# Hash attention and a gated feed-forward block: turning the first pair's second half of queries behind the first scores

## The chip, the cores and the metric

The kernel runs on one core of one Trainium2 chip. The metric is the device time of one execution in microseconds (us). The profile is of one execution; its times run from the first instruction of the span. TensorE is PE in the profile (its weight loads PEld), VectorE is DVE, ScalarE is ACT, GpSimd is POOL, SyncE, which issues most of the DMAs, is SP.

## The reference

Attention in which a query sees only the keys of its own hash bucket, and a feed-forward block behind it, all in 32-bit floats:

```python
q, k, v: (4, 8, 768, 64); proj: (64, 6); w_in: (512, 2048); w_out: (2048, 512)
q_bits = (einsum('bhsd,dk->bhsk', q, proj) > 0)      # six signs for a query, and k_bits for a key
mask = q_bucket[:, :, :, None] == k_bucket[:, :, None, :]
scores = where(mask, 1/sqrt(64) * q @ k.T, -1e9)
attn = softmax(scores)                               # with 1e-9 added to the sum
x = (attn @ v) as (3072, 512)
h = x @ w_in
out = (h / (1 + exp(-1.702 * h))) @ w_out            # (3072, 512)
```

## The kernel before, in words

Attention runs first, over 16 pairs of heads: a pair holds two heads of 64 rows each, so together they fill the 128 partitions. The sequence of 768 is cut into two halves `c` of 384 queries (`HS`) and six tiles `kt` of 128 keys; `GT` is 3, and `low` and `high` are key tiles 0 to 2 and 3 to 5. The feed-forward block behind it forms its matrix products from seven products of quarters with sums around them (L712 and L824 are its matmuls). A second, general version of the attention stands under a condition at the end and isn't taken here.

The order of the instructions on TensorE, VectorE, ScalarE and GpSimd is the order in which the code issues them (`manual_schedule`); the framework adds the waits. SP's DMA queue has its own order, which is the same in both kernels.

What the change touches is the start. `first_pair` handles pair 0, whose data are laid out in another way than the later pairs':

- It loads `k`, `proj` and `q` on the queues of SP and ScalarE, and lets TensorE run four `warm` matmuls (L359) meanwhile. `hash_weights` (L130, L133) makes the hash weights `pf_k` and `pf_q` from `proj` on VectorE.
- `turned(name, c, move)` turns a half of the keys or queries with matmuls against the identity (`tp`, L366: six matmuls, which the profile shows as 12 records), and the function `move` copies the result into `kT` or `qT` (L368). For `k` that is VectorE, for `q` ScalarE.
- `bits(name, c)` multiplies a half with the hash weights (`hash`, L373), and VectorE turns the signs into the features `kf` or `qf` (L374).
- `measure` (L398) sums the squares of a raw tile on ScalarE; a guard uses them at the end.

Then `scores(n, c, kts)` makes a score tile `ps` for each key tile (L432): two bf16 matmuls with the features, which add a large number where a bit agrees, and two 32-bit ones with `qT` and `kT`, one for each head. ScalarE takes the exponential into `e` (L433). `add_low` (L440, L441, POOL) and `add_high` (L446, L448, VectorE) sum the exponentials in `acc`, `values` multiplies them with `v` (`av`, L458), and `unload` (L469, L470) copies the result. From pair 1 on, `fetch` (L328) loads keys and queries, `turn` (L391) transposes them on VectorE, and `hashed` (L408) and `featured` (L413, with DMAs at L420 that bring the features into place) do the hashing.

Two sets of buffers tie these steps together. The pool `sps` has three score buffers in PSUM, used in turn by every `tp` of pair 0, every `hash` of pair 0 and every `ps`: a new one has to wait until the engine that reads the one three before it is done. And the raw queries of a pair have one buffer (pool `ld`, one buffer for each name), so `fetch(1, "q")` can't start before the last reader of pair 0's raw queries.

The main sequence, before:

```python
rest = first_pair()
fetch_v(0)
for x in "kq":
    fetch(1, x)
scores(0, 0, low)
rest()
```

Of the kernel before, what the change touches and what calls it, by code (L numbers as in the profile page):

```python
# [38 lines left out]
def kernel(  # L39
# [17 lines left out]
    nc = tc.nc  # L57
# [65 lines left out]
    def hash_weights():  # L123
        for x in "kq":
            for j in range(2):
                rows = slice(D * j, D * (j + 1))
                for h, sign in enumerate(SIGNS[x]):
                    c0 = NB * (2 * j + h)

                    nc.vector.scalar_tensor_tensor(pf[x][rows, c0 : c0 + NB], pj[rows], sign, ones[rows, 0:NB],  # L130
                                                   op0=Alu.mult, op1=Alu.mult)
            w, one = (y[:, 0 : 4 * NB].rearrange("p (j n) -> p j n", j=2) for y in (pf[x], ones))
            nc.vector.tensor_tensor(pf0[x][:, :, 0 : 2 * NB], w, one, op=Alu.mult)  # L133
# [149 lines left out]
    def attention(ff):  # L283
# [4 lines left out]
        with actx:  # L288
# [41 lines left out]
            def fetch_v(n):  # L330
                b, hp = pairs[n]
                x = ld.tile([P, T, 2, D], F32, tag="v", name="v", bufs=2)
                if n == 0:
                    x = x.rearrange("p t j d -> p (t j d)").rearrange("p (j t d) -> p t j d", j=2, d=D)
                vts[n] = x
                if n == 1:
                    behind(x[:, 0, :, 0])
                for j in range(2):
                    order = "(t p) d -> p t d" if n else "(p t) d -> p t d"
                    loader[0].dma_start(out=x[:, :, j, :], in_=v[b, 2 * hp + j].rearrange(order, p=P))  # L340

            def first_pair():


                b, hp = pairs[0]
                x = {}
                for i, (name, src) in enumerate((("k", k), ("q", q))):
                    raw = raws[0, name] = ld.tile([P, S // 32, 32], F32, tag=name, name=name)
                    x[name] = raw.rearrange("p s i -> p (s i)").rearrange("p (j t d) -> p j t d", j=2, d=D)
                    for j, queue in enumerate((nc.sync, nc.scalar)):  # L350
                        queue.dma_start(out=x[name][:, j], in_=src[b, 2 * hp + j].rearrange("(p t) d -> p t d", p=P))
                    if i == 0:
                        for j, queue in enumerate((nc.sync, nc.scalar)):
                            queue.dma_start(out=pj[D * j : D * (j + 1)], in_=proj)
                    xts[0, name] = wk.tile([P, S], F32, tag=f"{name}T", name=f"{name}T")

                nc.scalar.activation(const.tile([1, 1], F32, name="first"), ones[0:1, 0:1], Act.Exp)
                for _ in range(4):
                    nc.tensor.matmul(aps.tile([P, 512], F32, tag="av", name="warm"), idle[:, 0:P], idle, start=True, stop=True)  # L359
                hash_weights()  # L360

                def turned(name, c, move):
                    tp = sps.tile([P, 2, 512], F32, tag="s", name="tp")[:, 0, 0:HS]
                    for i in range(GT):
                        for j in range(2):
                            nc.tensor.matmul(tp[D * j : D * (j + 1), i * P : (i + 1) * P], x[name][:, j, c * GT + i, :], ident,  # L366
                                             start=True, stop=True)
                    move(xts[0, name][:, c * HS : (c + 1) * HS], tp)  # L368

                def bits(name, c):  # L370
                    cols = slice(c * HS, (c + 1) * HS)
                    h = sps.tile([P, 2, 512], F32, tag="s", name="hash0")[:, 0, 0:HS]
                    nc.tensor.matmul(h, pf0[name].rearrange("p j d -> p (j d)"), xts[0, name][:, cols], start=True, stop=True)  # L373
                    nc.vector.tensor_scalar(feats[0][name][:, cols], h, above0[name][:, 0:1], FEAT[name],  # L374
                                            op0=Alu.is_gt, op1=Alu.mult)

                measure(0, "k")
                turned("k", 0, nc.vector.tensor_copy)
                turned("k", 1, nc.vector.tensor_copy)
                turned("q", 0, nc.scalar.copy)  # L380
                turned("q", 1, nc.scalar.copy)
                measure(0, "q")
                bits("k", 0)
                bits("q", 0)
                bits("k", 1)
                return lambda: bits("q", 1)

            def turn(n, name):
                x = raws[n, name]
                xt = xts[n, name] = wk.tile([P, S], F32, tag=f"{name}T", name=f"{name}T")  # L390
                nc.vector.transpose(xt, x.rearrange("p s i -> p (s i)"))  # L391

            def measure(n, name):

                x = raws.pop((n, name))
                i = 2 * n + "kq".index(name)
                junk = st.tile([P, S], BF16, tag="junk", name="junk", bufs=1)
                nc.scalar.activation(junk, x.rearrange("p s i -> p (s i)"), Act.Square, accum_out=sizes[:, i : i + 1])  # L398
# [24 lines left out]
            def scores(n, c, kts):  # L423
                qT, kT, qf, kf = xts[n, "q"], xts[n, "k"], feats[n % 2]["q"], feats[n % 2]["k"]
                cols = slice(c * HS, (c + 1) * HS)
                for kt in kts:
                    ps = sps.tile([P, 2, 512], F32, tag="s", name="ps")
                    keys = slice(kt * P, (kt + 1) * P)
                    for a, m, last in ((kf, qf, False), (kT, qT, True)):
                        for j in range(2):  # L430
                            hs = slice(D * j, D * (j + 1))
                            nc.tensor.matmul(ps[:, j, 0:HS], a[hs, keys], m[hs, cols], start=not last, stop=last)  # L432
                    nc.scalar.activation(es[c][:, kt, :, 0:HS], ps[:, :, 0:HS], Act.Exp, scale=1.0 / D**0.5)  # L433
# [3 lines left out]
            def add_low(n, c):  # L437

                acc = accs[n, c, 0] = st.tile([P, 2, HS], F32, tag="acc0", name="acc0", bufs=1)
                nc.gpsimd.tensor_tensor(acc, es[c][:, 0, :, 0:HS], es[c][:, 1, :, 0:HS], op=Alu.add)  # L440
                nc.gpsimd.tensor_tensor(acc, acc, es[c][:, 2, :, 0:HS], op=Alu.add)  # L441
# [81 lines left out]


            low, high, every = range(GT), range(GT, T), range(T)
            rest = first_pair()
            fetch_v(0)
            for x in "kq":
                fetch(1, x)
            scores(0, 0, low)  # L530
            rest()
            add_low(0, 0)
            scores(0, 0, high)
            turn(1, "k")
            measure(1, "k")
            values(0, 0, low)
# [442 lines left out]

    ff = feed_forward("", in_chunks[len(in_chunks) - LATE :])  # L980
    attention(ff)
    whole(ff)
    fixed.close()
# [41 lines left out]
```

## Time and profile before

| what | value |
|---|---|
| time, median of 4 runs | 875.17 us (874.86 to 875.98) |
| the profiled execution | 875.0 us; its span 873.2 us |
| granted TensorE clock | 0.996 |
| TensorE matmuls | 861.7 us busy, 99% of the span |
| VectorE, ScalarE, GpSimd | 82%, 36%, 37% of the span |
| first score matmul (L432) | starts at 10.47 us |
| first values matmul (L458) | starts at 16.38 us |

The times of a timeline row are its start and its length; a row can merge several instructions (x12 means twelve). In square brackets stands how long the engine had been idle before, and who released it. The ends of matmuls are modelled, so rows of TensorE that follow each other overlap a little. The chain of waits is the chain of work that ended last, followed back from the end of the program; its pieces don't overlap, and "issue" in it is time in which an engine waited for nothing that the profile shows.

### The profile page before, as it was taken

The page shows a single profiled execution, that of the slowest core. Times are in us where ns is not written, and L with a number is a line of the kernel's source. Part 1 is how long each engine was busy: PE and PEld are TensorE (multiplying, and loading weights), DVE is VectorE, ACT ScalarE, POOL GpSimd, SP SyncE. Part 2 cuts the span into 40 slices and gives each one's busy share as a digit, 9 for nine tenths or more (in the row PEclk, how much of TensorE's full clock was granted, in tenths as well). Part 3 has the DMA queues.
Part 4 walks back from the last instruction along what each step waited for, and adds up shares of the span by engine and source line. Part 5 has one row for each costly group of instructions (what it writes and reads, how often), then busy time and mean ns, then how long its engine had stood idle before and what let it go on. Part 6 is the DMA issues. An engine that isn't in the chain of part 4 may idle for free.

```text
span 873.2 us, 11818 instructions
## 1 busy us (share of the span) xinstructions
PE 861.7 (99%) x4077; PEld 500.7 (57%) x4077; DVE 718.7 (82%) x1020; ACT 311.6 (36%) x519; POOL 321.2 (37%) x275
## 2 busy tenths in 40 slices
PE   9999999999999999999999999999999999999995
PEld 4444444444444444444444444444888888888884
DVE  4579999988999988778777778888888977897785
ACT  5756567777666653222233222332000000000000
POOL 4243334334433375665543344659903100000000
PEclk9999999999999999999999999999999999999998
DMA  5334456554445304565455545575844685467524
GB/s 133 59 59 84 84 104 101 116 88 83 84 84 91 75 25 158 192 217 193 175 193 186 205 180 196 190 251 179 299 168 156 199 247 197 166 200 241 193 97 99
DMA packets 169155, 131.99 MB, mean 151 GB/s; under 512 B 123616, under 2 KB 138112, under 8 KB 163712
## 3 DMA queue, kind: packets, MB, share of 16 engines
q1 hardware_dynamic: 166528, 129.70, 51.2%
q10 hardware_dynamic: 2560, 1.46, 0.7%
q8 instruction: 34, 0.56, 0.3%
q14 instruction: 33, 0.27, 0.1%
HBM read 79.69 MB, written 50.33 MB: 149 GB/s over the span
## 4 chain that ended last, share of the span: by engine, by line
PE 95%; DVE 3%; DMA 0%; issue 0%; ACT 0%; ACTq 0%; SPq 0%; DVEq 0%
PE product L712 33%; PE product L824 27%; PE ps L432 18%; PE av L458 14%; PE dn L479 1%; PE hash L408 1%; DVE xT L828 1%; DVE y L804 1%; DMA pj<-in_proj_dram 0%; DVE acc L448 0%; DVE xT L499 0%; PE hash L373 0%; DVE acc L446 0%; ACT e L433 0%; DVE v L828 0%
## 5 line engine op out<-in xcount | busy, mean ns | idle before, releaser
L433 ACT ACTIVATE e<-ps 128x768 f32<-128x768 f32 x192 | 150.2, 812 | 17.0 <-PE ps L432 14.9
L432 PE MATMUL ps<-qT,kT 64*128 64x384 f32 x768 | 155.1, 482 | 0.0
L712 PE MATMUL product<-xT,w_in_sb 128*128 128x512 f32 x288 | 135.4, 592 | 0.0
L458 PE MATMUL av<-e,v 128*64 128x385 f32 x768 | 128.2, 488 | 0.0
L440 POOL TENSOR_TENSOR acc<-e 128x768 f32<-128x768 f32 x32 | 51.2, 1599 | 192.2 <-ACT e L433 122.6
L720 ACT ACTIVATE c<-c 128x512 f32<-128x512 f32 x72 | 45.3, 630 | 185.0 <-issue 78.6
L458 PEld LDWEIGHTS av<-e,v 128*64 128x64 f32 x768 | 53.8, 136 | 72.9 <-issue 72.0
L712 PEld LDWEIGHTS product<-xT,w_in_sb 128*128 128x128 f32 x288 | 54.6, 190 | 69.0 <-issue 64.0
L712 PE MATMUL product<-t_x,s_in 128*128 128x512 f32 x192 | 90.2, 592 | 0.0
L432 PEld LDWEIGHTS ps<-qT,kT 64*128 64x128 f32 x768 | 68.0, 187 | 38.0 <-issue 37.5
L219 POOL TENSOR_TENSOR v<-c,u 128x512 f32<-128x512 f32 x24 | 34.1, 1422 | 121.2 <-ACT c L720 121.2
L837 ACT COPY u<-product 128x256 f32<-128x256 f32 x21 | 7.8, 372 | 172.1 <-PE product L824 138.9
L441 POOL TENSOR_TENSOR acc<-acc,e 128x768 f32<-128x768 f32 x32 | 64.0, 2001 | 2.5
L432 PE MATMUL ps<-qf,kf 64*128 64x384 bf16 x384 | 62.8, 324 | 0.1
L712 PEld LDWEIGHTS product<-t_x,s_in 128*128 128x128 f32 x192 | 36.5, 190 | 45.9 <-issue 43.8
L446 DVE SCALAR_TENSOR_TENSOR acc<-e 128x768 f32<-128x768 f32 x32 | 50.6, 1582 | 5.1 <-ACT e L433 5.1
L712 PE MATMUL product<-t_x,w_in_sb 128*128 128x512 f32 x96 | 45.1, 592 | 0.0
L712 PE MATMUL product<-xT,s_in 128*128 128x512 f32 x96 | 45.1, 592 | 0.0
L432 PEld LDWEIGHTS <-kf 64*128 64x128 bf16 x384 | 19.3, 94 | 35.2 <-issue 11.7
L448 DVE TENSOR_TENSOR acc<-acc,acc 128x768 f32<-128x768 f32 x32 | 31.2, 974 | 4.8 <-POOL acc L441 1.6
L824 PE MATMUL product<-raw_g,xT 128*128 128x256 f32 x152 | 35.1, 379 | 0.0
L448 DVE TENSOR_TENSOR acc<-acc,e 128x768 f32<-128x768 f32 x32 | 31.8, 995 | 3.8 <-ACT e L433 0.5
(207 smaller groups left out, 1494.0 us busy)
## 6 DMA issues: line engine op xcount, KB each, us to landing
raw_g<-g_dram SPq DMA_DIRECT2D x22, 1024.0 KB
s_in<-g_dram SPq DMA_DIRECT2D x20, 1024.0 KB
g_dram<-c SPq DMA_DIRECT2D x72, 256.0 KB
g_dram<-t SPq DMA_DIRECT2D x48, 256.0 KB
raw<-in_moe_w_in_dram SPq DMA_DIRECT2D x16, 512.0 KB
raw<-in_moe_w_out_dram SPq DMA_DIRECT2D x16, 512.0 KB
v<-in_v_dram SPq DMA_DIRECT2D x32, 192.0 KB
g_dram<-u SPq DMA_DIRECT2D x24, 256.0 KB
```

What stands on the lines that cost most here:

```text
L219: return [lambda: eng.tensor_tensor(t1, b12, b11, op=Alu.subtract), lambda: eng.tensor_tensor(b12, b22, b12, op=Alu.subtract), lambda: eng ...
L408: nc.tensor.matmul(h[r0 : r0 + 32, :], pf[x], xts[n, x][:, c * HS : (c + 1) * HS], start=True, stop=True)
L432: nc.tensor.matmul(ps[:, j, 0:HS], a[hs, keys], m[hs, cols], start=not last, stop=last)
L433: nc.scalar.activation(es[c][:, kt, :, 0:HS], ps[:, :, 0:HS], Act.Exp, scale=1.0 / D**0.5)
L440: nc.gpsimd.tensor_tensor(acc, es[c][:, 0, :, 0:HS], es[c][:, 1, :, 0:HS], op=Alu.add)
L441: nc.gpsimd.tensor_tensor(acc, acc, es[c][:, 2, :, 0:HS], op=Alu.add)
L446: nc.vector.scalar_tensor_tensor(acc, e[0], T * TINY, e[1], op0=Alu.add, op1=Alu.add)
L448: nc.vector.tensor_tensor(acc, acc, x, op=Alu.add)
L458: nc.tensor.matmul(av[D * j : D * (j + 1), :], vt[:, t, j, :], es[c][:, t, j, :], start=(t == 0), stop=(t == T - 1))
L712: nc.tensor.matmul(ps, wq[LEFT[i]][:, kc, :], xq[RIGHT[i]][:, kc, :], start=(kc == 0), stop=(kc == K2 - 1))
L720: nc.scalar.activation(c, c, Act.Gelu_apprx_sigmoid)
L824: nc.tensor.matmul(ps, wq[LEFT[i]][:, c, :], gq[RIGHT[i]][:, c, :], start=(c == 0), stop=(c == F4 - 1))
```

## The change

The second half of pair 0's queries is no longer turned in `first_pair`, ahead of the hashes. `first_pair` now returns two functions. The first turns that half behind the first three score tiles, and its copy into `qT` goes to VectorE instead of ScalarE. The second hashes that half and stands behind the next three score tiles, where before it stood behind the first three. The number of matmuls and copies is the same.

```diff
                 turned("k", 0, nc.vector.tensor_copy)
                 turned("k", 1, nc.vector.tensor_copy)
                 turned("q", 0, nc.scalar.copy)
-                turned("q", 1, nc.scalar.copy)
                 measure(0, "q")
                 bits("k", 0)
                 bits("q", 0)
                 bits("k", 1)
-                return lambda: bits("q", 1)
+
+                return lambda: turned("q", 1, nc.vector.tensor_copy), lambda: bits("q", 1)
...
-            rest = first_pair()
+            rest_turned, rest_hashed = first_pair()
             fetch_v(0)
             for x in "kq":
                 fetch(1, x)
             scores(0, 0, low)
-            rest()
+            rest_turned()
             add_low(0, 0)
             scores(0, 0, high)
+            rest_hashed()
             turn(1, "k")
             measure(1, "k")
             values(0, 0, low)
```

The raw queries of pair 0 are now read by TensorE after `fetch(1, "q")` stands in the code; the framework makes that load wait for them.

## The prediction

> **What bounds the kernel now.** I read the page's totals first, then TensorE's waits over the whole span, then the first 32 us of the timeline engine by engine, because everything that the diff touches lies there.
>
> From the page, busy time by engine, and the engines' shares of the chain of work that ended last:
>
> ```profile
> PE 861.7 (99%) x4077; PEld 500.7 (57%) x4077; DVE 718.7 (82%) x1020; ACT 311.6 (36%) x519; POOL 321.2 (37%) x275
> ...
> PE 95%; DVE 3%; DMA 0%; issue 0%; ACT 0%; ACTq 0%; SPq 0%; DVEq 0%
> ```
>
> The waits of TensorE over the whole span (who waited for whom: us in total, times, longest):
>
> ```profile
> PE warm L359 <- DVE idle L76: 1.2, 1, 1.2
> PE dn L479 <- DVE acc L448: 0.3, 1, 0.3
> PE tp L366 <- DVE kT L368: 0.3, 1, 0.3
> ```
>
> TensorE is the bound, and it is almost never held. So a change of order pays only as far as it removes idle time of TensorE, and costs only where it makes TensorE wait. Here is what the chain of waits shows of the affected stretch (start us, us, what):
>
> ```profile
> 7.33 0.88 PE tp L366 x12
> 8.21 1.50 PE hash L373 x4
> ...
> 9.80 0.63 DVE qf L374
> ...
> 10.47 2.60 PE ps L432 x18
> 13.07 0.84 PE hash L373 x2
> 13.92 2.53 PE ps L432 x18
> 16.45 2.09 PE av L458 x12
> ```
>
> From 7.33 us on this is one unbroken row of TensorE work, with one gap: after the hash of the first half of queries (ends 9.71) the scores wait for VectorE's `qf` (0.09 us of issue, 0.63 of work, 0.04 of issue). The hash of the second half of keys runs under that gap (9.53 for 0.81 us), so TensorE itself idles only from about 10.34 to 10.47, 0.13 us. The other idle time is the 0.3 us of the wait list, just before 7.33: `tp` of the second half of queries needs the score buffer that VectorE's first `kT` copy sets free.
>
> **The change, part by part.** Removed ahead of the first scores: 12 transpose records (`tp`, six matmuls of two records each; 0.88 us) and ScalarE's second `qT` copy (0.48 us). Added behind the first three score tiles: the same 12 records, and a copy on VectorE. Moved: the second-half hash (2 records, 0.84 us) and its `qf` (0.62 us), from behind the first three score tiles to behind the next three.
>
> *TensorE's sum.* At 7.33 the new head of the queue is the key hash; it needs the first `kT` copy, the event that ended the wait before as well. The row of work then reads: hash 1.50, `qf` and issue 0.76, scores 2.60, `tp` 0.88, scores 2.53, hash 0.84 = 9.11 us, and `av` at 16.44. Before it was 0.88 + 1.50 + 0.76 + 2.60 + 0.84 + 2.53 = 9.11: the same six terms in another order. The first scores start 0.88 earlier (9.59 for 10.47), the late transposes at 12.19, the second three score tiles at 13.07 for 13.92, the moved hash at 15.60, and `av` and everything behind it stand where they stood. Both idle pieces stay: the hash waits for the same `kT`, the scores for the same `qf`. Sum: 0.
>
> *Small terms that the trace doesn't settle.* The key hash needs an extra 51 ns event instruction (the profile has two of them on L373, at 7.8 and 7.9, hidden under the transposes); now they stand behind a wait: 0 to +0.10, I take +0.05. Changes between half-height matmuls (scores) and full-height ones (transposes, hash, `av`) cost 0.10 each (scores tile to tile 0.81 apart, scores to hash 0.91): four before, four after, 0. From below: if both idle pieces vanished, -0.43.
>
> [...] The weight-load row shows each transpose loading for 137 ns, and twelve of them with their loads in 0.88 us. [...] I take the row, and keep +0.33 for the range.
>
> *Clock.* The transposes' rows (duration min/median/max):
>
> ```profile
> L366 PE MATMUL tp<-ident,k x24: 273/421/472, 3.7 to 6.0; 128*64 128x128 f32 x24
> ...
> L366 PE MATMUL tp<-ident,q x24: 272/273/323, 6.2 to 7.9; 128*64 128x128 f32 x24
> ```
>
> The same instruction runs at 421 ns up to about 6 us and at 273 after, at a granted clock of 1.00 throughout. The scores, 0.88 earlier, still start 3.4 us after that step (9.59 against 6.17). [...] By the row 0; I take 0.
>
> *The ring of three score buffers* now ties TensorE to other engines in new places, and each has slack. The transposes reuse the first score tile's buffer: its exponential is done at about 11.4 (from 10.6, three in 2.43), wanted at 12.2. The fourth score tile needs the second exponential (12.2, wanted 13.1), the fifth the third (13.1, wanted 13.9), the sixth VectorE's copy (0.51, from 13.1 to 13.6, wanted 14.7), the hash the fourth (14.9, wanted 15.6). Least slack 0.7. The copy itself is free: VectorE sat idle 2.96 us before 13.96.
>
> *VectorE behind the moved hash.* Its queue, timeline rows:
>
> ```profile
> 13.96 0.62 DVE L374 TENSOR_SCALAR qf<-hash,above_q 128x384 bf16<-128x384 f32 x1 [2.96 <-PE hash L373]
> 14.49 0.97 DVE L391 STREAM_TRANSPOSE kT<-k 128x768 f32<-128x768 f32 x1
> ...
> 19.54 0.97 DVE L391 STREAM_TRANSPOSE qT<-q 128x768 f32<-128x768 f32 x1
> 24.01 0.68 DVE L413 TENSOR_SCALAR f<-hash,above,weight 128x384 bf16<-128x384 f32 x1 [3.50 <-PE hash L408]
> ```
>
> `qf` now starts at about 16.5; behind it queue the transpose of pair 1's keys (to 18.1), three `acc` steps of 0.96 to 1.05 (to 21.1) and the transpose of its queries (to 22.1). TensorE asks for `qf` at 18.46 (ready 17.1), and for pair 1's `kT` and `qT` at 23.09: 1.0 us of slack. The load of pair 2's keys waits for that first transpose and for ScalarE's `measure`: 18.1, where it started at 18.16.
>
> *The load of pair 1's queries* fills the buffer that the late transposes read, so in the built program it waits on SP for a TensorE count that now includes them (43 for 28 matmuls). Its four DMA issues:
>
> ```profile
> 9.59 2.02 SPq L328 DMA_DIRECT2D q<-in_q_dram x4
> 18.16 2.02 SPq L328 DMA_DIRECT2D k<-in_k_dram x4
> ```
>
> They move from 9.59 to about 13.1. Next in SP's queue is the second row, at 18.1, so nothing is pushed. The like load of keys keeps the DMA engines busy from 18.2 to about 21.7, 3.5 us from its first issue; so the queries are in by 16.7, wanted by VectorE at 21.1. ScalarE's and POOL's DMA and compute order are otherwise unchanged; POOL's `acc` simply starts 0.9 earlier.
>
> **The rivals.**
>
> *1, nothing moves (likeliest).* +0.05 us against the profiled execution's 875.0 (873.2 of span and 1.8 around it). The median of the runs is 0.17 above that execution: 875.17 + 0.05 = 875.2.
>
> *2, faster.* Scores 0.88 earlier would pay if ScalarE were the limit later on. Against it: its exponentials had waited 0.96 for TensorE at 14.88, and TensorE never waits for ScalarE in the list above. The two idle pieces together bound the gain at 0.43: 874.7, still inside 0.2%. To pass 0.2% it needs idle time that the records hide.
>
> *3, slower: pair 1's queries come too late.* One mechanism: the held load, behind it the `qT` transpose on VectorE, behind that the hash at L408 (23.09), which heads TensorE's in-order queue. It decides from the point where that transpose starts after 22.1, so if the load lands 5.4 us later than I work out, or VectorE's queue slips by 1.0. Then each us late is a us of the total; the feature DMAs behind `f`, needed at 30.43, would hold further. A load landing at 24.5 gives +2.4: 877.6. For it: the 1.0 of slack on VectorE is the smallest of the case's long ones. Against it: the DMA engines have nothing else from 13.1 to 18.1, and VectorE's steps have measured durations.
>
> *4, the change doesn't do what it says:* the transposes stay held until something of the second score group. The order of the built program puts them right behind the third score tile, with one wait, on the first exponential; so I give it little, and its time would be rival 1's plus at most 0.7.
>
> **How the numbers follow.** No change (1, with 4): 0.90. Faster (2, beyond its bound): 0.04. Slower (3): 0.06. A measurement of this kernel can tell about 0.2%, 1.75 us, from no change; so faster 0.04, same 0.90, slower 0.06. The unknown costs reach from -0.43 to +0.6 (0.10 + 0.33, and two extra changes of height at 0.10); the four runs shown lie from 0.3 below to 0.8 above their median. 875.17 - 0.43 - 0.3 gives 874.4, 875.17 + 0.6 + 0.8 gives 876.6. Both ends are inside rival 1.
>
> **What would show it.** Right: first `ps` at about 9.6, `tp` of queries at 12.2 with no wait on ScalarE, the last hash of L373 at about 15.6, `av` at 16.4 to 16.6, `hash` L408 at 23.1 to 23.3, from there the old rows. Wrong: a TensorE wait on `e`, on `qT` at L408, or on the feature DMAs before 30.4; or `av` more than 0.5 us from 16.4; or key hashes longer than 0.5 us per record.

## The result: 1.1 us faster, and the profile after

The changed kernel takes 874.19 us (median of 32 runs, 873.12 to 875.31), the kernel before 875.28 us in the runs beside it (52 runs, 874.45 to 876.34). The ratio is 0.9987, 95% interval 0.9983 to 0.9992: 0.7 to 1.5 us faster. That is within the 0.2% that the prediction called no change, but it is clear of the noise of these runs, and the time lies 0.2 us below the predicted range. The profiled execution took 873.7 us, its span 871.9 us for 873.2.

The page's totals of the changed kernel show nothing of it: the work of TensorE is the same to 0.1 us.

```profile
PE 861.7 (99%) x4077; PEld 500.6 (57%) x4077; DVE 719.4 (83%) x1021; ACT 311.9 (36%) x518; POOL 321.3 (37%) x275
```

The chain of waits at the start of the changed kernel (start us, us, what):

```profile
7.20 1.51 PE hash L373 x4
...
8.81 0.63 DVE qf L374
...
9.48 2.60 PE ps L432 x18
12.08 0.81 PE tp L366 x12
12.88 2.53 PE ps L432 x18
15.41 0.84 PE hash L373 x2
16.25 2.09 PE av L458 x12
```

From the start of the hashes to `av` it takes 9.05 us. Before it took 9.12 from the start of the transposes that stood first there. So the reordered start is worth what the sum said, nothing; the 0.2 us by which `av` comes earlier is the start itself, which differs from execution to execution (`av` lies between 15.80 and 17.19 us in the profiles of this study, leaving out the one with 64 more memsets, which delay the start). The wait of 0.3 on `kT` goes with the start too: `proj` landed earlier here (VectorE begins on it at 4.99 for 5.35), and in the first experiment below, where it landed at 4.03, the wait is missing in the old order as well.

Where TensorE waits, over the whole span of the changed kernel (the full answer):

```profile
PE warm L359 <- DVE idle L76: 1.2, 1, 1.2
```

One more wait of before is missing: `dn` L479 on VectorE's `acc`. It stands at 50.96 us, far behind everything that the change moves. What led to it, VectorE's timeline in the kernel before:

```profile
39.98 0.92 DVE L446 SCALAR_TENSOR_TENSOR acc<-e 128x768 f32<-128x768 f32 x1
41.42 0.96 DVE L448 TENSOR_TENSOR acc<-acc,e 128x768 f32<-128x768 f32 x1 [0.53 <-ACT e L433]
```

and in the changed kernel:

```profile
39.78 0.92 DVE L446 SCALAR_TENSOR_TENSOR acc<-e 128x768 f32<-128x768 f32 x1
40.81 0.96 DVE L448 TENSOR_TENSOR acc<-acc,e 128x768 f32<-128x768 f32 x1
```

The second step follows the first after 0.52 us in the one (41.42 less 40.90) and after 0.11 in the other (40.81 less 40.70). The releaser in brackets, an exponential, is misleading: the tile that this step reads was ready at 36.3 (its row of six exponentials starts at 31.53 and takes 4.79). In the trace's own records the event instruction between the two steps ends at 40.95, and nothing runs on VectorE for the next 0.47 us. From there to 50.91 every VectorE step follows the one before it within 0.1 us, so the delay reaches TensorE, which gets the sums late:

```profile
49.82 0.84 PE L479 MATMUL dn<-acc,ones 128*32 128x384 f32 x4
50.96 0.84 PE L479 MATMUL dn<-acc,ones 128*32 128x384 f32 x4 [0.30 <-DVE acc L448]
```

In the changed kernel the same eight records are one row without a wait:

```profile
49.62 1.59 PE L479 MATMUL dn<-acc,ones 128*32 128x384 f32 x8
```

The third difference is at the very end. From the last VectorE transpose (865.40 before, 864.83 after) to the end of the span it takes 7.80 us before and 7.09 after. In the event records, all engines but VectorE pass the program's closing barrier at 871.9 in the kernel before; VectorE's event follows at 872.85 and holds the second round of that barrier. In the changed kernel all pass at 871.33. Between the two, from 872.29 to 872.65, runs a fetch of instructions (a DMA record of 8192 bytes on the queue that the page lists as `q14 instruction`; the record doesn't say for which engine). In the changed kernel the last such fetch starts at 871.35, when VectorE has passed.

So of 1.28 us between the two spans, 0.20 is the start, 0.39 the stretch from `dn` of pair 0 to that of pair 2 (34.84 us before, 34.45 after), 0.71 the end, and the 795 us between, by far the most of the program, differ by 0.02.

What the stop at 41 us and the late end have in common is VectorE's instruction stream. The change gives VectorE one instruction more (the `qT` copy), so every later VectorE instruction stands one place further on. In the built program the `acc` step that stopped is number 64 of VectorE's stream (counted from 0; the trace lacks one branch ahead of it), and 65 after the change. The theory that follows, P: the gain comes from this shift alone. The rival, O: it comes from the order, the scores that start earlier.

### The profile page after: what moved, and what is told of

Same layout as the page of the kernel before. It is cut to its first block, busy times and chain, and to the rows that moved or that the text cites. A ratio compares the mean times of both kernels' runs of the same rounds, so it can differ in the third digit from the quotient of the medians.

```text
span 871.9 us, 11818 instructions
## 1 busy us (share of the span) xinstructions
PE 861.7 (99%) x4077; PEld 500.6 (57%) x4077; DVE 719.4 (83%) x1021; ACT 311.9 (36%) x518; POOL 321.3 (37%) x275
## 4 chain that ended last, share of the span: by engine, by line
PE 97%; DVE 2%; issue 0%; ACTq 0%; ACT 0%; DVEq 0%
PE product L713 33%; PE product L825 27%; PE ps L432 18%; PE av L458 15%; PE dn L479 2%; PE hash L408 1%; DVE xT L829 1%; DVE y L805 1%; PE tp L366 0%; PE warm L359 0%; PE hash L373 0%; DVE v L829 0%; DVE t2a L221 0%; DVE raw_g L220 0%; ACTq L812 0%
## 5 line engine op out<-in xcount | busy, mean ns | idle before, releaser
L433 ACT ACTIVATE e<-ps 128x768 f32<-128x768 f32 x192 | 150.8, 812 | 16.5 <-PE ps L432 14.2
L446 DVE SCALAR_TENSOR_TENSOR acc<-e 128x768 f32<-128x768 f32 x32 | 50.6, 1581 | 4.0 <-ACT e L433 4.0
L448 DVE TENSOR_TENSOR acc<-acc,acc 128x768 f32<-128x768 f32 x32 | 31.2, 974 | 4.8 <-POOL acc L441 1.6
L448 DVE TENSOR_TENSOR acc<-acc,e 128x768 f32<-128x768 f32 x32 | 31.8, 995 | 3.3
```

The costliest lines, as they stand in the source:

```text
L446: nc.vector.scalar_tensor_tensor(acc, e[0], T * TINY, e[1], op0=Alu.add, op1=Alu.add)
L448: nc.vector.tensor_tensor(acc, acc, x, op=Alu.add)
```

## The experiments

All times are medians; ratios are against the kernel before in the same rounds. Lines of code are those of the kernel that is named.

**One VectorE instruction more, nothing else.**

```diff
     nc.vector.memset(ones, 1.0)
+    nc.vector.memset(ones, 1.0)
```

> The kernel before with one more VectorE instruction: the memset of the ones tile is issued twice, at 1.1 us, where VectorE has nothing else to do until the projection lands at about 5 us. No order changes. Theory P (place in the instruction stream: the change gains because it puts one instruction more on VectorE ahead of the acc step at 41 us, so that a 0.47 us stop at that step and a 0.9 us late VectorE at the final barrier go): about 874.2, ratio 0.9987 to 0.9990, no TensorE wait at dn L479, and VectorE not last at the final barrier. Theory O (order: the scores that start 0.9 us earlier bring the gain): nothing changes, ratio 1.000.

Measured: 874.12 for 875.54 us, ratio 0.9985 (0.9976 to 0.9994). A memset that does nothing, in idle time, brings all that the change brings. VectorE's timeline of this kernel (its L447 and L449 are L446 and L448 of before) shows the stop gone:

```profile
39.40 0.92 DVE L447 SCALAR_TENSOR_TENSOR acc<-e 128x768 f32<-128x768 f32 x1
40.42 0.96 DVE L449 TENSOR_TENSOR acc<-acc,e 128x768 f32<-128x768 f32 x1
```

From the last transpose to the end 6.93 us. Theory O falls with this run, unless the order brings something as well.

**The changed order without the shift, in two ways.** The copy of the late half goes back to ScalarE:

```diff
-                return lambda: turned("q", 1, nc.vector.tensor_copy), lambda: bits("q", 1)
+                return lambda: turned("q", 1, nc.scalar.copy), lambda: bits("q", 1)
```

> The changed kernel with the copy of the late-turned queries back on ScalarE, so the order of TensorE is the changed one and the number of VectorE instructions is that of before. Theory P: ratio 1.000 plus or minus 0.0003, about 875.2, the 0.47 us stop of the acc step at about 41 us and the late VectorE at the final barrier are back. Theory O: as the changed kernel, 874.2, ratio 0.9987.

Measured: 875.91 for 875.54 us, 1.0002 (0.9993 to 1.0011). From the waits of TensorE in this kernel:

```profile
PE dn L479 <- DVE acc L448: 0.3, 1, 0.3
```

The wait at `dn` is back, and so is the late VectorE at the end (7.85 us from the last transpose). And the changed kernel as it is, copy on VectorE, with one memset at the start moved off VectorE:

```diff
-        nc.vector.memset(pf[x], 0.0)
+        (nc.vector if x == "k" else nc.gpsimd).memset(pf[x], 0.0)
```

> The changed kernel with one VectorE instruction less at the start (the memset of the query hash weights on POOL), so its order is the changed one, copy on VectorE included, and every later VectorE instruction has the place it had before. Theory P: 1.000 plus or minus 0.0004 against the kernel before (about 875.5), with the 0.47 us stop of the acc step and the late VectorE at the end. Theory O: as the changed kernel, 0.9987.

Measured: 875.10 for 875.29 us, 1.0003 (0.9994 to 1.0012); stop, `dn` wait and late end (7.66 us) all there. VectorE's timeline:

```profile
39.94 0.92 DVE L446 SCALAR_TENSOR_TENSOR acc<-e 128x768 f32<-128x768 f32 x1
41.38 0.96 DVE L448 TENSOR_TENSOR acc<-acc,e 128x768 f32<-128x768 f32 x1 [0.53 <-ACT e L433]
```

So with the old places the new order brings no gain that these runs can tell.

**The changed kernel and the one memset more, side by side.**

> The changed kernel itself, on the same chip and in the same rounds as the others. Both theories: 0.9985 to 0.9989. Against the next one it measures what the order is worth at equal places: theory P says within 0.3 us of it.

> The kernel before with the memset of the ones tile issued twice, again, beside the changed kernel. Theory P: 0.9984 to 0.9989, within 0.3 us of the changed kernel. Theory O: 1.000.

Measured: the changed kernel 873.94 us, 0.9988 (0.9979 to 0.9997); the kernel before with the memset twice 874.38 us, 0.9991 (0.9982 to 1.0000); 875.29 before. The two kernels differ by 0.44 us where theory P said at most 0.3: a miss, though the difference is smaller than the width of either interval (0.0018, or 1.6 us). So the order may still be worth some tenths, in either direction, which these runs don't settle.

**The two parts one by one.** A VectorE instruction more behind the stop and ahead of the end (it writes one element of a hash weight tile that nobody reads any more):

```diff
             next(ff)
+            nc.vector.memset(pf0["k"][0:1, 0, 0:1], 0.0)
             whole(invert(last))
```

> The kernel before with one tiny VectorE memset (one element of a hash weight tile that is no longer read) at the end of the attention, behind the stop at 41 us and ahead of the end. Theory P, if its two parts are separate: the stop at 41 us and the dn wait of 0.3 us stay, the late VectorE at the final barrier goes: about 874.5, ratio 0.9991 to 0.9993. Theory O: 1.000.

Measured: 874.35 for 875.54 us, 0.9986 (0.9977 to 0.9995). The stop and the wait stay, the end is 7.07 us. TensorE's timeline of this kernel at the two `dn`:

```profile
50.12 0.84 PE L479 MATMUL dn<-acc,ones 128*32 128x384 f32 x4
51.27 0.84 PE L479 MATMUL dn<-acc,ones 128*32 128x384 f32 x4 [0.32 <-DVE acc L448]
```

That is more of a gain than forecast, though the interval takes in 0.9993; in the profile the end is worth 0.73 (7.80 less 7.07). The times alone don't tell this one part from both parts; the profiles do. And a VectorE instruction less at the start, the memset of the query weights on POOL in the kernel before:

```diff
-        nc.vector.memset(pf[x], 0.0)
+        (nc.vector if x == "k" else nc.gpsimd).memset(pf[x], 0.0)
```

> The kernel before with one VectorE instruction less at the start: the memset of the query hash weights moves from VectorE to POOL, in a time where both are idle. Theory P: the stop moves by one instruction the other way, behind the acc step, where that step's 0.96 us covers it, so the dn wait goes (0.3 to 0.4 us); what the final barrier does isn't known, since the last instructions move the other way too: if VectorE stays late there, ratio 0.9995 to 0.9997 (about 874.9), if not, 0.9988. Theory O: 1.000.

Measured: 875.06 for 875.54 us, 0.9997 (0.9988 to 1.0006), which by itself can't be told from no change. The profile can: no stop, no `dn` wait, but the end at 7.92 us. VectorE's timeline:

```profile
39.82 0.92 DVE L446 SCALAR_TENSOR_TENSOR acc<-e 128x768 f32<-128x768 f32 x1
40.84 0.96 DVE L448 TENSOR_TENSOR acc<-acc,e 128x768 f32<-128x768 f32 x1
```

VectorE is again the engine that passes late, one instruction further on: its event at 871.45 is in time, and its next instruction (a DRAIN in the records) comes only at 872.43.

**How wide is the step?**

```diff
     nc.vector.memset(ones, 1.0)
+    for _ in range(40):
+        nc.vector.memset(ones[0:1, 0:1], 1.0)
...
                 bits("k", 1)
+                for _ in range(23):
+                    nc.vector.memset(ones[0:1, 0:1], 1.0)
```

> The kernel before with 64 more VectorE instructions, tiny memsets of one element (and one event instruction), 40 before the projection lands and the others between the last early key feature and the next query feature, where VectorE idled 2.96 us. If the place in the stream matters in steps of 64 instructions, everything is as before: stop of 0.47 us at the acc step, VectorE late at the end, ratio 1.000. [...] A pure question of the chip's step; theory O has no word on it but 1.000.

Measured: 875.16 for 875.29 us, 0.9998 (0.9989 to 1.0007). The total misleads: the memsets, one every 0.11 us, hold VectorE until the hash weights are 1.2 us late (6.56 for 5.35), and `av` starts at 17.51. The stop is gone, the `dn` wait too, the stretch between the `dn` is 34.42 us and the end 7.11. So 64 places are not a full step. Then 128 and 127 more, in five idle times of VectorE ahead of 36 us: at the two places of the last run and behind `turn(1, "q")`, `fetch_v(1)` and `turn(2, "k")`, with 25 (or 24), 22, 28, 30 and 23 memsets:

> The kernel before with 128 more VectorE instructions, tiny memsets of one element spread over five idle times of VectorE ahead of 36 us. One look, for its profile: its total isn't compared, since the memsets may delay the start. If the step of the stream is 128 instructions, the acc step stands where it stood and the stop of 0.47 us is back there, TensorE waits 0.3 us at dn L479, 34.8 us pass from the first dn to that of the pair after the next, and VectorE is late at the final barrier (7.7 to 7.9 us from the last VectorE transpose to the end). If only the one place mattered: no stop, 34.4 us, 7.0 us.

> The same with 127 more. With a step of 128 it is in the place of the kernel with one VectorE instruction less: no stop at the acc step, no dn wait, 34.4 us, but VectorE late at the end, 7.7 to 7.9 us.

Each was measured in one execution, so only the profiles are read. With 128 more, VectorE's timeline (L450 and L452 there) has the stop again, 0.40 us in the records, and the `dn` wait:

```profile
40.38 0.92 DVE L450 SCALAR_TENSOR_TENSOR acc<-e 128x768 f32<-128x768 f32 x1
41.75 0.96 DVE L452 TENSOR_TENSOR acc<-acc,e 128x768 f32<-128x768 f32 x1 [0.46 <-ACT e L437]
```

```profile
PE dn L483 <- DVE acc L452: 0.2, 1, 0.2
```

The end is late too. With 127 more all is as with one less: no stop, and a late end.

All profiles together, read from the trace's records (place: that of the `acc` step in VectorE's stream; then the gap ahead of that step, the time from the first `dn` of pair 0 to that of pair 2, and from the last VectorE transpose to the end, in us):

| kernel | place | gap | dn to dn | end |
|---|---|---|---|---|
| before | 64 | 0.47 | 34.84 | 7.80 |
| changed, copy on ScalarE | 64 | 0.48 | 34.85 | 7.85 |
| changed, one less | 64 | 0.47 | 34.85 | 7.66 |
| before, one more late | 64 | 0.48 | 34.85 | 7.07 |
| before, 128 more | 192 | 0.40 | 34.79 | 7.86 |
| before, one less | 63 | 0.05 | 34.43 | 7.92 |
| before, 127 more | 191 | 0.05 | 34.43 | 7.74 |
| changed | 65 | 0.05 | 34.45 | 7.09 |
| changed again | 65 | 0.05 | 34.44 | 7.01 |
| before, one more | 65 | 0.05 | 34.43 | 6.93 |
| before, one more again | 65 | 0.05 | 34.43 | 7.02 |
| before, 64 more | 128 | 0.05 | 34.42 | 7.11 |

Every column follows from the number of VectorE instructions ahead, whichever order the start has: the gap ahead of this step is there at places 64 and 192 and at no other, and the end is long when the whole stream has as many instructions as before, one less, or 127 or 128 more.

The same step of 128 shows inside single streams, at an instruction that no edit aimed at. L198 writes `w_out_sb`, weights of the feed-forward block, and follows directly on a short event instruction, as the `acc` step does. In the kernel before, one of these instructions stands at place 831:

```profile
505.10 1.06 DVE L195 TENSOR_TENSOR w_out_sb<-bits,part 128x512 f32<-128x512 f32 x1
506.26 1.05 DVE L198 SCALAR_TENSOR_TENSOR w_out_sb<-size,w_out_sb 128x512 f32<-128x512 f32 x1
```

In the changed kernel it stands at 832, which is 64 + 6 x 128, and has a stop of its own:

```profile
504.51 1.06 DVE L195 TENSOR_TENSOR w_out_sb<-bits,part 128x512 f32<-128x512 f32 x1
506.03 1.04 DVE L198 SCALAR_TENSOR_TENSOR w_out_sb<-size,w_out_sb 128x512 f32<-128x512 f32 x1 [0.46 <-DVE w_out_sb L195]
```

In the records the gap behind the event is 0.40 us for 0.04. This instruction comes 16 times in each kernel, 192 times in the twelve profiles. In eight of the profiles one of them stands at place 832 or (before, one less) 704, which is 64 + 5 x 128, and there the gap is 0.40 us; at the other 184, places 705, 831 and 833 among them, it is 0.04. No wait of TensorE goes with these stops. So the change took away a stop that TensorE felt and brought one that it doesn't feel.

## Why the prediction was right and wrong

**Right: TensorE's sum at the start.** The six terms measured 1.51, 0.77, 2.60, 0.81, 2.53 and 0.84, together 9.06 of the 9.11 forecast. From the start of the hashes to `av` it takes 9.05 to 9.07 us in all four profiles with the new order, and 8.24 in all with the old one, where the transposes stand ahead of the hashes. The difference of about 0.82 is the moved block: what the scores gain at their start, the moved transposes take back in full. The same for the covers: the late transposes at 12.01 (12.19 forecast), the copy at 12.93 (13.1), the load of pair 1's queries at 12.96 (13.1), `qf` at 16.29 (16.5) and the hash L408 at 22.89 (23.1) all stood where they were put, 0.1 to 0.2 us earlier with the start, and no wait of TensorE came with them; rival 3, the late queries, had no trace. The transposes' step from 421 to 273 ns cost nothing either: in the records it is over at 6.46 us, ahead of the first hash at 7.13. Its cause isn't shown: the trace's record of the granted clock begins only there, at 6.45 us (5.92 before), so the 1.00 that the prediction gives ahead of the step rests on no record.

**Not shown, without effect: the 0.33 us for weight loads.** The prediction kept this term for its range; no run shows it. Full-height blocks stand behind half-height scores twice in both kernels: the hash (13.00) and `av` (16.38) before, the transposes (12.01) and the hash (15.34) after. What the runs show in its place is the switch itself: from the start of a score tile to such a block 0.90 to 0.92 us in both kernels, to another score tile 0.81. The transposes take 0.81 us from their start to the start of what follows in both kernels (7.33 to 8.14, 12.01 to 12.81); the 0.88 of the timeline row includes the modelled end of the last of them.

**Wrong: "The copy itself is free", and that `av` "and everything behind it stand where they stood".** The copy's 0.56 us are free. But it is an instruction, and the prediction counted what instructions cost where they stand, not what they move. One more on VectorE moved the `acc` step at 41 us off a place where the engine stops, and its last instructions off places where it passes the closing barrier late. Measured, that term is 0.4 (34.84 to 34.44) plus 0.7 (7.8 to 7.1), 1.1 us, where the sum had 0; it accounts for the whole of the result, within what the runs can tell. The step that failed is the listing of what the copy does: it named VectorE's idle time at 13 us as the cover, and looked no further along VectorE's queue than the hash at 23 us. That the gain stayed under 0.2% all the same, as "no change" had it, was luck as far as the copy goes: no term of the sum bounded it.

**Wrong: the bound from below.** The range went down only by the idle time of TensorE that the change touches (0.43). The wait list shown in the prediction had a third wait, 0.3 us at `dn` L479, and it was left out of the bound without a reason. It went. And the 7.8 us between the last VectorE transpose and the end of the span had no term in the sum. Rival 2 asked for "idle time that the records hide", and that is what it was, in part.

**What stays open.** That the place in the stream decides is shown; what the engine does in the 0.4 us is not. That it goes on to its next stretch of instructions is a guess: the fetches on q14 are of 8192 bytes, and no run shows how many instructions one of them holds. A fetch goes with the place, too: of the two nearest the stop, the earlier one starts at 39.0 to 39.9 us in the four profiles with place 65, and at 42.0 to 42.9 in the seven with places 63, 64, 191 and 192. But in the kernel before both start behind the stop, at 42.2 and 42.4, and no DMA packet of any queue runs from 40 to 42 us; so the stop isn't the time of a fetch. The late end may be one: in all six profiles with a long end a fetch runs after the other engines have passed, and ends 0.1 to 0.5 us ahead of VectorE's late record. Why only some of these places show a stop isn't shown either: all the stops that were found stand behind an event instruction of 21 ns, while at places 192, 320 and 448 of the kernel before, where the engine goes directly from one step of 0.7 to 2.0 us to the next, nothing shows (the next step starts 0.08 us ahead of the end of the one before it). That the running step covers a stop there is a guess.

## What to carry to other kernels

An edit that adds or removes one instruction on an engine moves all later ones of that engine, and a stop of the kind seen here on VectorE (0.40 to 0.48 us, at places a multiple of 128 apart) can thereby turn up, go, or move to where it costs nothing. So before a tenth of a per cent is put down to an edit's logic, measure the kernel before with an idle instruction added and with one taken away. Split the difference of two spans at a few marks (first result, a mid stage, last compute, end): here the two parts that made the difference (0.39 and 0.71 us) lay far behind the code that was changed. And where the order on an engine that is always busy is changed, add up its terms in the old and in the new order: work that is only moved takes back later what it saves first.

## What was not expected of the hardware

VectorE's stream has places at which it stops for 0.40 to 0.48 us, multiples of 128 instructions apart (64, 192, 704 and 832 in these profiles, not 128). One place earlier or later the same instruction shows nothing of a stop (0.04 or 0.05 us), and the profile can put a stop down to an engine that had long been done (the one from 40.95 us on in the kernel before, to an exponential done at 36.3). The length of the whole stream decides the end in a like way: from the last VectorE transpose it takes 7.66 to 7.92 us where VectorE passes the closing barrier late, and 6.93 to 7.12 where it doesn't, since the other engines go on only when VectorE has passed (in the kernel before they pass the first round at 871.9 us, VectorE at 872.85, and all the second at 873.1).
